# Key halves copied from PSUM into the score slots, wide mask transposes and a new order in a block-sparse attention and Hyena kernel

## The chip, the cores and the metric

The kernel runs on one core of a Trainium2 chip. The metric is the device time of one execution in microseconds. Before the change the median of three executions is 249.28 us (249.26 to 249.30). The profiled execution has a span of 248.8 us.

In what follows PE is TensorE, ACT is ScalarE, DVE is VectorE, POOL is GpSimd and SP is SyncE, which issues all the DMAs.

## The reference

Two stages follow each other. The first is causal attention in which every query sees its own block of 64 keys and the three blocks with the highest gate scores; the second is a Hyena layer with an FFT over the sequence and a product of three projections.

```python
batch, n_heads, seq, head_dim = (4, 8, 768, 64); block = 64; top_k = 3
k_rep = k.reshape(B, H, n_blocks, block, D).mean(axis=3)
gate_scores = np.einsum('bhsd,bhnd->bhsn', q, k_rep)          # blocks after the query's own: -1e9
top_idx = np.argsort(gate_scores, axis=-1)[..., -top_k:]
# mask: keys of the chosen blocks and of the own block, and no key after the query
scores = np.where(mask, scale * np.matmul(q, k.transpose(0, 1, 3, 2)), -1000000000.0)
x = np.matmul(softmax(scores), v)                              # then [B, S, H * D]
proj = x @ w_proj                                              # x1, x2, x3
x2_conv = np.fft.irfft(np.fft.rfft(x2, axis=1) * np.fft.rfft(filter_fft, axis=0), n=S, axis=1)
out = (x1 * x2_conv * x3) @ w_out
```

## The kernel before

The work on attention is cut into 16 pairs of heads (`g`), four pairs to a batch. Each pair goes through `prep(g)` and `attn(g)`; when four pairs are done, `hyena(b)` can work on their batch. `filt()` prepares the Fourier matrices and the filter once, at the start.

`prep` works so. The loads (L274, L281) bring k, q and v of two heads into tiles kn, qn and vn, with the sequence on the partitions. Six transposes `kT` (L342) put both heads' keys into PSUM, in two halves of 384 columns, so that head 0 has partitions 0 to 63 and head 1 has 64 to 127. DVE sums each block of 64 keys (`ks`, L345), and ACT copies the 384 columns as 16-bit numbers into a tile k2 (`k2`, L350). Six transposes `qT` (L374) do the same for q; ACT writes the scaled high part q2h (L377) and DVE the remainder q2l (L380). POOL splits the key sums into a high and a low part (`km`, L363, L364). Twenty small matmuls `gate` (L409) give the gate scores. DVE then finds the third largest of each row (`max`, L422 to L428) and compares (`lt`, L434, L439); the result nm says which blocks are not chosen. Five transposes `mT` (L450) turn nm, and a copy `md` (L458) puts 12 rows of it for each head beneath the q of that head.

The score slots kt and qt are the operands of the score matmuls `sc` (L480). For each head, rows 0 to 63 hold k and q; rows 64 to 75 of kt hold a constant pattern (-30720 in the columns of one block), and the same rows of qt hold nm. So one matmul with 76 rows gives the scores with the unchosen blocks pushed far down. Because head 1 sits on partitions 64 to 127 after the transposes but is needed on 0 to 63, `shuffle` (L393) moves the halves of k2 and q2h into the slots by DMA. For the first two pairs engines copy instead (L395).

`attn` runs, for each head, three pieces of scores with two PSUM banks each (`sc`), an exponential on ACT (`ex`, L486), a causal cut on POOL (`sel`, L491), and 21 matmuls with v (`pv`, L508); DVE normalises (`rec` L517, `nrm` L521, tile xn). Then a DMA transposes xn into xT (L540), sums and differences of xn (`eo`, L546) go through the Fourier matrices (`st1`, L558, L565), and copies of that are XT (L571).

`hyena` has, per batch, six groups `s2` of four matmuls (L667) on the four pairs' XT; DVE multiplies each group's PSUM twice with the filter (`t`, L676) and the sums Y (L686) are made on DVE or POOL. Sixteen groups `x13` (L703) are the projections, `prod` (L712) their product, `cv` (L730) the transform back, then `sd` (L745), `yT` (L751), and six groups `op` (L761) with the copy `osb` (L765) and the store.

The order is a planned one. `build` makes a graph of operations, each with a due time `vt`, the engines that could do it and a cost on each. `plan` then runs through a model of five engines, PSUM banks and buffer pools, and always takes the operation that could start soonest, or, of those nearly equal, the one due first. While PE would have nothing to do in the first 30 us of the plan, it adds filler matmuls (L856)[...]. What comes out is a fixed sequence for each engine, and each engine keeps to it: an instruction that waits holds up all that stands behind it on its engine, on SP's DMA queue as well. A few numbers in `PAR` shift the due times, and `POOLS` says how many buffers each tile has.

Of the kernel before, what the change touches and what calls it, by code (L numbers as in the profile page):

```python
# [24 lines left out]
KR = D + NB  # L25
# [16 lines left out]
for _pi, _segs in enumerate(PIECES):  # L42
# [6 lines left out]
    p0=-2.579, p1=0.077, a0=0.0, pvlag=0.294, dlag=1.997, dlen=0.945, h0=5.459, hlen=3.658, f0=0.196,  # L49
    f1=4.432, ld=-1.443, s2a=-0.205, s2b=0.422, x0=0.488, x1=0.938, c0=0.578, c1=0.847, o0=1.481,  # L50
    o1=1.0, pen_dve=0.221, ahead=2.229, delta=0.029, queue=6.554, direct=2, late=2.0, w0=1.031, wl=1.656,
    wlag=-0.256, warm_until=30, tr0=-7.197, trl=1.834, fill0=0.703,
)

POOLS = dict(kn=3, qn=3, vn=2, k2=2, q2h=2, q2l=2, ks=2, km=3, m8=2, nm=2,
# [8 lines left out]
class Buf:  # L64
    def __init__(self, pool):
        self.pool, self.slot, self.left = pool, None, 0
        self.w, self.r = {}, {}
        self.free = self.busy = 0.0
        self.users = []
# [7 lines left out]
class Graph:  # L77
    def __init__(self):
        self.ops = []

    def add(self, tag, vt, eng, emit, rd=(), wr=(), res=(), lock=False, size=0):
        o = Op()
        o.i, o.tag, o.vt, o.eng, o.emit, o.lock, o.size = len(self.ops), tag, vt, eng, emit, lock, size
# [25 lines left out]
def pe_cost(mms):  # L109
    occ = sum(mms)  # L110
    return occ, occ - mms[-1] + 0.17 + mms[-1]


def dve(n, rate=1.0):
    occ = n / (960.0 * rate) + 0.066
    return occ, occ + 0.15
# [11 lines left out]
def build(par):  # L128
    g_ = Graph()
# [56 lines left out]
    add("phase", T0, {"DVE": (1.0, 1.15)}, e_phase, wr=[cb("phase"), cb("magic")])  # L186
    add("iota", T0 + .1, {"POOL": pol(1.7)}, e_iota, wr=[cb("cols")])
    add("nyq", T0 + .2, {"DVE": (0.08, 0.23)}, e_nyq, wr=[cb("cols")])
    def e_eblk(E, nc, en):
        nc.gpsimd.memset(E.eblk[64:KR, :], EMASK)  # L190
        nc.gpsimd.affine_select(out=E.eblk[64:KR, :], in_=E.eblk[64:KR, :], compare_op=ALU.is_ge,
                                fill=0.0, base=0, pattern=[[1, S]], channel_multiplier=-64)
        nc.gpsimd.affine_select(out=E.eblk[64:KR, :], in_=E.eblk[64:KR, :], compare_op=ALU.is_ge,
                                fill=0.0, base=63, pattern=[[-1, S]], channel_multiplier=64)

    add("eblk", T0 + 3, {"POOL": pol(2.5)}, e_eblk, wr=[cb("eblk")])


    slot_init = []
    for i in range(POOLS["kt"]):  # L200
        def e_fill(E, nc, en, i=i):
            eng = nc.vector if en == "DVE" else nc.gpsimd
            eng.memset(E.t["qt"][i][64:KR, :, 0:P], 0.0)
            eng.tensor_copy(
                E.t["kt"][i][64:KR, :, :],
                E.eblk[64:KR, :].rearrange("p (o s) -> p o s", o=1).to_broadcast([NB, 2, S]))
        slot_init.append(add("fill", par["fill0"] + i, {"DVE": (0.62, 0.77), "POOL": pol(2.6)}, e_fill, rd=[cb("eblk")],
                             wr=[cb(("slot", i))]))

    def e_small(E, nc, en):  # L210
        for t_ in E.t["km"]:
            nc.vector.memset(t_, 0.0)
        for t_ in E.t["nm"]:
            nc.vector.memset(t_, 0.0)
        for t_ in E.t["va"]:
            nc.vector.memset(t_[:, :, :, 64:65], 1.0)
        nc.vector.memset(E.crow, 2.0 / S)
        nc.vector.memset(E.crow[0:1, :], 1.0 / S)
# [47 lines left out]
    for g in range(NG):  # L266
# [4 lines left out]
        for n_, (src, dst) in enumerate((("k", kn[g]), ("q", qn[g]))):  # L271
            for t in range(2):
                def e_ld(E, nc, en, b=b, j=j, t=t, dst=dst, src=src):
                    nc.sync.dma_start(E.sb(dst)[:, :, t, :],  # L274
                                      getattr(E, src)[b, 2 * j + t].rearrange("(c p) d -> p c d", p=P))
# [48 lines left out]
    def prep(g):  # L324
        direct = g < par["direct"]
# [5 lines left out]
        Kt[g], Qt[g] = Buf("kt"), Buf("qt")  # L331
        if g < POOLS["kt"]:
            Kt[g].slot = Qt[g].slot = g
        k2, q2h, q2l, ks, km = Buf("k2"), Buf("q2h"), Buf("q2l"), Buf("ks"), Buf("km")
        m8, nm = Buf("m8"), Buf("nm")
        for hf in range(2):
# [11 lines left out]
            def e_k2(E, nc, en, cs=cs, kp=kp):  # L348
                if en == "ACT":
                    nc.scalar.copy(E.sb(k2)[:, cs], E.bk(kp)[:, 0:HS])  # L350
                else:
                    nc.vector.tensor_copy(E.sb(k2)[:, cs], E.bk(kp)[:, 0:HS])

            add("kT", v(.0 + .1 * hf), {"PE": pe_cost([0.109] * 3)}, e_kt, rd=[(kn[g], 0), (kn[g], 1), cb("id32")], wr=[kp],
                res=[k2, ks])
            add("ks", v(.05 + .1 * hf), {"DVE": dve(HS)}, e_ks, rd=[kp], wr=[(ks, hf)])
            add("k2", v(.05 + .1 * hf), {"ACT": act(HS)}, e_k2, rd=[kp], wr=[(k2, hf)])

        def e_km(E, nc, en):
            for t in range(2):  # L360
                r = slice(64 * t, 64 * t + 64)
                cc = slice(12 * t, 12 * t + 12)
                nc.gpsimd.tensor_copy(E.sb(km)[r, 0, cc], E.sb(ks)[r, :])  # L363
                nc.gpsimd.tensor_tensor(E.sb(km)[r, 1, cc], E.sb(ks)[r, :], E.sb(km)[r, 0, cc],  # L364
                                        op=ALU.subtract)

        add("km", v(.3), {"POOL": pol(1.0)}, e_km, rd=[(ks, 0), (ks, 1), cb("small")], wr=[km])
        for hf in range(2):
            cs = slice(HS * hf, HS * (hf + 1))
            qp = psb()  # L370

            def e_qt(E, nc, en, hf=hf, qp=qp):
                for c in range(HC):
                    nc.tensor.transpose(E.bk(qp)[:, P * c:P * (c + 1)], E.sb(qn[g])[:, HC * hf + c, :, :], E.id32)  # L374

            def e_qh(E, nc, en, cs=cs, qp=qp):
                nc.scalar.activation(E.sb(q2h)[:, cs], E.bk(qp)[:, 0:HS], AF.Copy, bias=0.0, scale=QS)  # L377

            def e_ql(E, nc, en, cs=cs, qp=qp):
                nc.vector.scalar_tensor_tensor(out=E.sb(q2l)[:, cs], in0=E.bk(qp)[:, 0:HS], scalar=QS,  # L380
                                               in1=E.sb(q2h)[:, cs], op0=ALU.mult, op1=ALU.subtract)

            add("qT", v(.2 + .1 * hf), {"PE": pe_cost([0.109] * 3)}, e_qt, rd=[(qn[g], 0), (qn[g], 1), cb("id32")], wr=[qp],
                res=[q2h, q2l])
            add("qh", v(.25 + .1 * hf), {"ACT": act(HS)}, e_qh, rd=[qp], wr=[(q2h, hf)])
            add("ql", v(.27 + .1 * hf), {"DVE": dve(HS)}, e_ql, rd=[qp, (q2h, hf)], wr=[(q2l, hf)])

        def shuffle(src, dst, vt, tag):
            for t in range(2):
                def e_sh(E, nc, en, t=t):  # L390
                    o, i_ = E.sb(dst)[0:64, t, :], E.sb(src)[64 * t:64 * t + 64, :]
# [5 lines left out]
                add(tag, vt, eng, e_sh, rd=[(src, 0), (src, 1)], wr=[(dst, ("h", t))],  # L397
                    size=0 if direct else 98, lock=direct)

        shuffle(k2, Kt[g], v(.3), "shK")  # L400
        shuffle(q2h, Qt[g], v(.4), "shQ")

        gn = psb()

        def e_gate(E, nc, en):
            o = E.bk(gn)
            for c in range(1, NQ):
                for n_, (qx, w) in enumerate(((q2h, 0), (q2h, 1), (q2l, 0), (q2l, 1))):
                    nc.tensor.matmul(o[:, 32 * c:32 * c + 24], lhsT=E.sb(qx)[:, P * c:P * (c + 1)],  # L409
                                     rhs=E.sb(km)[:, w, 0:24], start=(n_ == 0), stop=(n_ == 3))  # L410

        add("gate", v(.5), {"PE": pe_cost([0.026] * 20)}, e_gate,
            rd=[(q2h, 0), (q2h, 1), (q2l, 0), (q2l, 1), km], wr=[gn], res=[m8, nm])
# [16 lines left out]
        def e_lt(E, nc, en):  # L430
            o = E.bk(gn)
            gv = o[:, 32:32 * NQ].rearrange("p (c n) -> p c n", n=32)
            n_ = E.sb(nm)
            nc.vector.tensor_tensor(n_[:, :, :, 0:NB],  # L434
                                    gv[:, :, 0:24].rearrange("p c (t n) -> p c t n", t=2),
                                    E.sb(m8)[:, :, :, 2:3].to_broadcast([P, 5, 2, NB]), op=ALU.is_lt)
            row = 5 * 2 * 32
            for half in range(2):
                nc.vector.memset(bass.AP(tensor=n_.tensor, offset=n_.offset + half * (64 * row + 1) + 2,  # L439
                                         ap=[[row, 64], [66, 5], [32, 2]]), 0.0)  # L440

        add("max", v(.55), {"DVE": (1.12, 1.25)}, e_max, rd=[gn], wr=[gn, m8])
        add("lt", v(.56), {"DVE": (0.53, 0.65)}, e_lt, rd=[gn, m8, cb("small")], wr=[nm])
# [3 lines left out]
        def e_mt(E, nc, en):  # L447
            o = E.bk(mt).bitcast(FP16)
            for c in range(5):
                nc.tensor.transpose(o[0:64, P * c:P * (c + 1)],  # L450
                                    E.sb(nm)[:, c, :, :].rearrange("p t n -> p (t n)"), E.id16)

        add("mT", v(.8), {"PE": pe_cost([0.056] * 5)}, e_mt, rd=[nm, cb("id16")], wr=[mt],
            res=[Qt[g]])
        for t in range(2):
            def e_md(E, nc, en, t=t):
                o = E.bk(mt).bitcast(FP16)
                (nc.vector.tensor_copy if en == "DVE" else nc.scalar.copy)(  # L458
                    E.sb(Qt[g])[64:KR, t, P:S], o[32 * t:32 * t + NB, 0:S - P])
            add("md", v(.85), {"DVE": (0.398, 0.55), "ACT": (0.59, 0.755)}, e_md, rd=[mt, cb(("slots", g))],  # L460
# [5 lines left out]
    def attn(g):  # L466
# [3 lines left out]
        for t in range(2):  # L470
            a = g + par["a0"] + 0.5 * t
            exs = []
            for pi in range(3):
# [3 lines left out]
                def e_sc(E, nc, en, t=t, pi=pi, sp=sp):  # L477
                    o = E.sp(sp)
                    for (col, kc, q0, w) in PIECES[pi]:
                        nc.tensor.matmul(o[:, col:col + w], lhsT=E.sb(Kt[g])[0:KR, t, P * kc:P * (kc + 1)],  # L480
                                         rhs=E.sb(Qt[g])[0:KR, t, q0:q0 + w], start=True, stop=True,
# [6 lines left out]
                def e_sel(E, nc, en, pi=pi, ex=ex):  # L488
# [7 lines left out]
                    rd=[(Kt[g], ("h", t)), (Qt[g], ("h", t)), (Qt[g], ("m", t)), cb(("slots", g))], wr=[sp], res=[ex])  # L496
# [3 lines left out]
            for n_, cs in enumerate(((0, 1, 2), (3, 4), (5,))):  # L500
# [11 lines left out]
                add("pv", a + par["pvlag"] + 0.05 * n_, {"PE": pe_cost([0.030] * sum(c + 1 for c in cs))},  # L512
# [548 lines left out]
```

## Time and profile before

| | before |
|---|---|
| median time | 249.28 us |
| span of the profiled execution | 248.8 us |
| busy PE / DVE / ACT / POOL | 236.4 / 204.8 / 175.6 / 129.3 us |
| share of PE in the chain that ended last | 79% |
| k copies on ACT (L350) | 32, 481 ns each |
| DMAs kt<-k, qt<-q2h | 28 and 28, 96 KB each, 3.0 and 3.5 us to landing |
| fillers (L856) | 106, 16.2 us busy |

A matmul's end is modelled in this profile, and matmuls are pipelined; a busy PE is therefore not a PE at its best, and the start of one group to the start of the next tells more. Times of an engine's idle stretch are given with the instruction that ended it.

### The profile page before, as it was taken

The page shows a single profiled execution, that of the slowest core. Times are in us where ns is not written, and L with a number is a line of the kernel's source. Part 1 is how long each engine was busy: PE and PEld are TensorE (multiplying, and loading weights), DVE is VectorE, ACT ScalarE, POOL GpSimd, SP SyncE. Part 2 cuts the span into 40 slices and gives each one's busy share as a digit, 9 for nine tenths or more (in the row PEclk, how much of TensorE's full clock was granted, in tenths as well). Part 3 has the DMA queues.
Part 4 walks back from the last instruction along what each step waited for, and adds up shares of the span by engine and source line. Part 5 has one row for each costly group of instructions (what it writes and reads, how often), then busy time and mean ns, then how long its engine had stood idle before and what let it go on. Part 6 is the DMA issues. An engine that isn't in the chain of part 4 may idle for free.

```text
span 248.8 us, 6695 instructions
## 1 busy us (share of the span) xinstructions
PE 236.4 (95%) x2410; PEld 161.1 (65%) x2410; DVE 204.8 (82%) x643; ACT 175.6 (71%) x296; POOL 129.3 (52%) x240
## 2 busy tenths in 40 slices
PE   8978998999889899999999999999999999999994
PEld 6756687678556576867766677677566766645651
DVE  7899788988997999998899786778898968589860
ACT  2877999999667679886865796767756873524443
POOL 6662457675485547554558476643444614063420
PEclk9999999999997999999999999999999999999999
DMA  6999499997999958999976895421415131032006
GB/s 167 336 229 249 102 248 221 233 245 174 275 212 224 234 151 203 247 180 214 216 188 172 195 279 115 107 54 33 108 42 161 42 34 32 9 139 109 3 20 234
DMA packets 98945, 40.02 MB, mean 161 GB/s; under 512 B 89440, under 2 KB 93024, under 8 KB 98912
## 3 DMA queue, kind: packets, MB, share of 16 engines
q1 hardware_dynamic: 98912, 39.60, 66.3%
q8 instruction: 19, 0.31, 0.5%
q14 instruction: 14, 0.11, 0.2%
HBM read 24.64 MB, written 6.29 MB: 124 GB/s over the span
## 4 chain that ended last, share of the span: by engine, by line
PE 79%; DVE 7%; SPq 6%; DMA 3%; ACT 2%; issue 1%; DVEq 0%; ACTq 0%
PE ps L703 16%; PE ps L480 14%; PE ps L761 8%; PE ps L667 8%; PE ps L508 7%; PE ps L730 6%; PE ps L558 4%; SPq L274 3%; PE ps L374 3%; PE ps L342 3%; PE ps L409 2%; PE ps L450 2%; PE ps L565 2%; SPq L297 2%; DMA t<-in_moe_w_out_dram 2%; DVE t L676 2%
## 5 line engine op out<-in xcount | busy, mean ns | idle before, releaser
L486 ACT ACTIVATE ex<-ps 128x1024 f16<-128x1024 f32 (+1 forms) x96 | 86.1, 930 | 14.7 <-PE ps L480 14.4
L491 POOL TENSOR_SCALAR_AFFINE_SELECT ex<-ex 128x256 f16<-128x256 f16 x96 | 41.7, 437 | 52.4 <-ACT ex L486 51.6
L480 PE MATMUL ps<-qt,kt 76*128 76x512 f16 (+3 forms) x256 | 51.2, 310 | 0.3 <-ACT ex L486 0.3
L703 PE MATMUL ps<-xT,wp 128*128 128x384 f16 x256 | 50.5, 326 | 0.0
L703 PEld LDWEIGHTS <-wp 128*128 128x128 f16 x256 | 24.0, 97 | 14.1 <-issue 0.2
L686 POOL TENSOR_TENSOR Y<-t,t 128x512 f16<-128x512 f32 (+1 forms) x18 | 23.4, 1306 | 18.7 <-DVE t L676 18.3
L480 PEld LDWEIGHTS <-kt 76*128 76x128 f16 x256 | 23.1, 99 | 15.1 <-issue 1.4
L508 PEld LDWEIGHTS <-ex 128*128 128x128 f16 x672 | 25.2, 97 | 3.9 <-POOL km L363 0.4
L508 PE MATMUL ps<-va,ex 128*128 128x65 f16 x672 | 26.8, 193 | 0.2 <-DVE nm L434 0.2
L765 ACT COPY osb<-ps 128x512 f32<-128x512 f32 x24 | 14.2, 590 | 15.1 <-PE ps L761 15.0
L667 PE MATMUL ps<-wp,XT 128*128 128x512 f16 x96 | 23.7, 381 | 0.2 <-DVE t L676 0.2
L761 PE MATMUL ps<-wo,yT 128*128 128x512 f16 x96 | 23.8, 379 | 0.0
L751 POOL TENSOR_TENSOR yT<-prod,sd 128x384 f16<-128x384 f32 x16 | 15.9, 1000 | 13.5 <-DVE sd L745 11.2
L712 DVE TENSOR_TENSOR prod<-ps,x 128x384 f32<-128x384 f32 x32 | 17.6, 552 | 6.5 <-PE ps L703 6.2
L350 ACT CAST k<-ps 128x384 f16<-128x384 f32 x32 | 14.7, 481 | 11.3 <-DVE colv L182 4.6
L676 DVE TENSOR_TENSOR t<-ps,HA 128x512 f32<-128x512 f32 x24 | 16.5, 686 | 6.3 <-PE ps L667 6.2
L730 PE MATMUL ps<-G,Y 128*128 128x384 f16 x96 | 20.8, 326 | 0.0
L709 ACT CAST x<-ps 128x384 f16<-128x384 f32 x29 | 14.0, 483 | 9.4 <-PE ps L703 4.6
L345 DVE TENSOR_REDUCE ks<-ps 128x6 f32<-128x384 f32 x32 | 17.1, 552 | 4.1 <-ACT k L350 2.0
L380 DVE SCALAR_TENSOR_TENSOR q2l<-ps,q2h 128x384 f16<-128x384 f32 x32 | 17.0, 551 | 2.3 <-ACT q2h L377 2.2
L521 DVE TENSOR_TENSOR xn<-ps,rec 128x384 f16<-128x384 f32 x32 | 17.8, 556 | 1.0
L745 DVE TENSOR_TENSOR sd<-ce,ps 128x384 f32<-128x384 f32 x32 | 16.3, 549 | 2.2 <-PE ps L730 1.5
(106 smaller groups left out, 435.0 us busy)
## 6 DMA issues: line engine op xcount, KB each, us to landing
kn<-in_k_dram SPq DMA_DIRECT2D x32, 192.0 KB, 3.6
qn<-in_q_dram SPq DMA_DIRECT2D x32, 192.0 KB, 3.6
vn<-in_v_dram SPq DMA_DIRECT2D x16, 384.0 KB, 4.3
out_dram<-osb SPq DMA_DIRECT2D x24, 256.0 KB, 2.0
t<-in_moe_w_proj_dram SPq DMA_DIRECT2D x12, 256.0 KB, 4.2
kt<-k SPq DMA_DIRECT2D x28, 96.0 KB, 3.0
qt<-q2h SPq DMA_DIRECT2D x28, 96.0 KB, 3.5
t<-in_moe_filter_fft_dram SPq DMA_DIRECT2D x6, 256.0 KB, 4.6
```

The lines of the kernel that those rows point to most:

```text
L480: nc.tensor.matmul(o[:, col:col + w], lhsT=E.sb(Kt[g])[0:KR, t, P * kc:P * (kc + 1)], rhs=E.sb(Qt[g])[0:KR, t, q0:q0 + w], start=True, sto ...
L486: nc.scalar.activation(E.sb(ex)[:, 0:w], E.sp(sp)[:, 0:w], AF.Exp, scale=ESC)
L491: nc.gpsimd.affine_select(out=dv, in_=dv, compare_op=ALU.is_ge, fill=0.0, base=0, pattern=[[0, 2], [1, P]], channel_multiplier=-1)
L508: nc.tensor.matmul(o[:, 65 * c:65 * c + 65], lhsT=E.sb(exs[pi])[:, col:col + P], rhs=E.sb(va[g])[:, t, kc, :], start=(kc == 0), stop=(kc = ...
L521: nc.vector.tensor_tensor(E.sb(xn)[:, :, t, :], pov[:, :, 0:64], E.sb(rec).rearrange("p (c n) -> p c n", n=1) .to_broadcast([P, NQ, D]), o ...
L667: nc.tensor.matmul(E.bk(xa), lhsT=w, rhs=E.wp[:, j, Dm:2 * Dm], start=(j == 0), stop=(j == NP - 1))
L676: nc.vector.tensor_mul(E.sb(dst), E.bk(xa), m)
L686: (nc.vector if en == "DVE" else nc.gpsimd).tensor_tensor(E.sb(Y)[ro, n_, :], E.sb(x)[ri, :], E.sb(y)[ri, :], op=op)
L703: nc.tensor.matmul(E.bk(xq)[:, 0:HS], lhsT=E.wp[:, d2, 2 * Dm * m + P * dc:2 * Dm * m + P * (dc + 1)], rhs=E.sb(xT[gs[d2]])[:, cs], start= ...
L712: nc.vector.tensor_mul(E.sb(prod)[:, cs], E.bk(xq)[:, 0:HS], E.sb(x1))
L730: nc.tensor.matmul(E.bk(cv)[:, 0:HS], lhsT=E.sb(Y)[:, 3 * p_ + n_, P * dc:P * (dc + 1)], rhs=E.G[:, 3 * p_ + n_, :], start=(n_ == 0), stop ...
L761: nc.tensor.matmul(E.bk(op_), lhsT=E.sb(yT)[:, d2, P * c:P * (c + 1)], rhs=E.wo[:, d2, :], start=(d2 == 0), stop=(d2 == NP - 1))
```

## The change

It has four parts.

1. Key halves: the score slots are laid out anew. Head 1, which leaves the transposes on partitions 64 to 127, keeps them, with its block pattern and mask in partitions 0 to 11; head 0 keeps 0 to 63 with pattern and mask in 64 to 75. So the keys can be copied from PSUM straight into the slot, one copy of 64 partitions for each head and half, on ACT or DVE, and no DMA moves them. The score matmul of head 1 has 128 rows (rows 12 to 63 are zero), that of head 0 still 76. The q halves still go by DMA, from a tile qx that holds high and low part, now into 128-column pieces.
2. Mask transposes: nm is one tile with 64 columns for each 128 queries, and each transpose takes 128 of them, so that the masks come out on the partitions where both heads need them.
3. km: POOL writes a copy more for each head, so that high and low part can be placed apart from where they are made.
4. Order: the planner's costs, due times and penalties are set anew, with a shift for each kind of operation, and buffers of kt, qt and qx are taken in the pairs' order. Pools: kn 3 to 2, k2 2 to 1 (unused), nm 2 to 1, q2h and q2l (2 each) become qx with 4.

The diff also carries another way to bring q (`by_dma`); with `tm=16` no pair uses it. `kin=16` makes all pairs take the new way for keys.

```diff
-KR = D + NB
+XW = 2 * P * NQ + 64
+NMW = 64 * NQ
+KR = (76, 128)
...
-    p0=-2.579, p1=0.077, a0=0.0, pvlag=0.294, dlag=1.997, dlen=0.945, h0=5.459, hlen=3.658, f0=0.196,
+    p0=-2.542, p1=0.159, a0=0.0, pvlag=0.294, dlag=1.721, dlen=1.15, h0=5.159, hlen=3.761, f0=-0.171,
...
-POOLS = dict(kn=3, qn=3, vn=2, k2=2, q2h=2, q2l=2, ks=2, km=3, m8=2, nm=2,
+POOLS = dict(kn=2, qn=3, vn=2, k2=1, qx=4, ks=2, km=3, m8=2, nm=1,
...
     def add(self, tag, vt, eng, emit, rd=(), wr=(), res=(), lock=False, size=0):
         o = Op()
+        vt += self.par.get("v_" + tag, 0.0)
...
+            if in_place:
+                for t in range(2):
+                    def e_k2(E, nc, en, hf=hf, kp=kp, t=t):
+                        r = slice(64 * t, 64 * t + 64)
+                        (nc.scalar.copy if en == "ACT" else nc.vector.tensor_copy)(
+                            E.sb(Kt[g])[r, HC * hf:HC * (hf + 1), 1 - t, :],
+                            E.bk(kp)[r, 0:HS].rearrange("p (c s) -> p c s", s=P))
+                    add("k2", v(.05 + .1 * hf + .02 * t), {"ACT": act(HS), "DVE": dve(HS)} , e_k2, rd=[kp],
+                        wr=[(Kt[g], ("h", t, hf))])
...
-                nc.gpsimd.tensor_copy(E.sb(km)[r, 0, cc], E.sb(ks)[r, :])
-                nc.gpsimd.tensor_tensor(E.sb(km)[r, 1, cc], E.sb(ks)[r, :], E.sb(km)[r, 0, cc],
-                                        op=ALU.subtract)
+                nc.gpsimd.tensor_copy(x[r, 2, 0:12], E.sb(ks)[r, :])
+                nc.gpsimd.tensor_tensor(x[ru, 1, cc], E.sb(ks)[r, :], x[r, 2, 0:12], op=ALU.subtract)
+                nc.gpsimd.tensor_copy(x[ru, 0, cc], x[r, 2, 0:12])
...
-                    o, i_ = E.sb(dst)[0:64, t, :], E.sb(src)[64 * t:64 * t + 64, :]
+                    r = slice(64 * t, 64 * t + 64)
+                    o = E.sb(dst)[r, :, 1 - t, :]
+                    i_ = E.sb(src)[r, col:col + S].rearrange("p (c s) -> p c s", s=P)
...
-        shuffle(k2, Kt[g], v(.3), "shK")
-        shuffle(q2h, Qt[g], v(.4), "shQ")
+        if not in_place:
+            shuffle(k2, 0, Kt[g], v(.3), "shK")
...
+            shuffle(qx, 0, Qt[g], v(.4), "shQ")
...
-                nc.tensor.transpose(o[0:64, P * c:P * (c + 1)],
-                                    E.sb(nm)[:, c, :, :].rearrange("p t n -> p (t n)"), E.id16)
+                nc.tensor.transpose(o[:, P * c:P * (c + 1)], E.sb(nm)[:, 64 * c:64 * c + P], E.id16)
...
-                        nc.tensor.matmul(o[:, col:col + w], lhsT=E.sb(Kt[g])[0:KR, t, P * kc:P * (kc + 1)],
-                                         rhs=E.sb(Qt[g])[0:KR, t, q0:q0 + w], start=True, stop=True,
+                        nc.tensor.matmul(o[:, col:col + w], lhsT=E.sb(Kt[g])[0:KR[t], kc, 1 - t, :],
+                                         rhs=E.sb(Qt[g])[0:KR[t], q0 // P:(q0 + w) // P, 1 - t, :],
+                                         start=True, stop=True,
...
-            add("rec", vt, {"DVE": (0.105, 0.25)}, e_rec, rd=pos, wr=[rec])
+            add("rec", vt, {"DVE": (0.2, 0.3)}, e_rec, rd=pos, wr=[rec])
```

## The prediction

> **What bounds the kernel now.** I read the page's engine shares and the slices first, then busy time by stage, then TensorE's own timeline where the stages show holes.
>
> ```profile
> span 248.8 us, 6695 instructions
> ...
> PE 236.4 (95%) x2410; PEld 161.1 (65%) x2410; DVE 204.8 (82%) x643; ACT 175.6 (71%) x296; POOL 129.3 (52%) x240
> ```
>
> 95% for PE is too kind: a pipelined matmul counts as busy until its modelled end, and 106 matmuls (L856, 16 us) are fillers. From start to start the timeline gives 0.65 us for four of x13 (L703), 0.67 for 21 of pv, 0.86 for four of s2 or op, 0.49 for 20 of gate or three of cv, 0.65 for six k or q transposes, 1.13 for one head's scores. Times their counts: x13 41.6, sc 36.3, pv 21.2, s2 and op 20.7 each, kT and qT 20.9, st1 15.8, cv 15.6, gate 8.0, mT 4.5, filter and trig 6: **about 211 us of real TensorE work**. The other 38 us of the span are fillers, a tail of about 4 us, and waiting. By stage (busy time of PE, PEld, DVE, ACT, POOL, then clock, DMA share, GB/s):
>
> ```profile
> 0.00:24.00 24.00, 19.82 (x174) 15.96 (x175) 21.00 (x71) 15.67 (x32) 13.90 (x27) 1.00 0.98 245
> 24.00:64.00 40.00, 38.61 (x535) 28.74 (x533) 33.73 (x141) 37.42 (x58) 23.99 (x57) 1.00 0.88 211
> 64.00:90.00 26.00, 22.86 (x221) 14.97 (x218) 23.53 (x74) 17.56 (x29) 15.52 (x29) 0.93 1.03 221
> 90.00:200.00 110.00, 110.00 (x1210) 75.83 (x1210) 94.38 (x302) 83.66 (x138) 61.41 (x114) 1.00 0.63 149
> 200.00:240.00 40.00, 40.00 (x263) 23.49 (x261) 31.06 (x57) 17.75 (x36) 14.49 (x15) 1.00 0.19 48
> ```
>
> Four regimes. To 24 us DVE and the DMA engines are full. From 24 to 64, the first four head pairs, ACT is 94% busy. From 64 to 90, where batch 0's s2 joins, DVE is 90% busy, PE has holes and the clock sinks. After 90 PE never stops: there about 152 us of work fill 155 us, and no change to the other engines can win anything. **So only the first 90 us can be shortened.** The holes of the third regime, on TensorE (start, length, what, idle before and who ended it):
>
> ```profile
> 65.98 0.44 PE L450 MATMUL ps<-id,nm 128*64 128x128 f16 x5 [0.80 <-DVE t L676]
> 66.45 2.75 PE L667 MATMUL ps<-wp,XT 128*128 128x512 f16 x12
> ...
> 70.93 1.02 PE L667 MATMUL ps<-wp,XT 128*128 128x512 f16 x4 [0.21 <-DVE t L676]
> 72.49 0.20 PE L409 MATMUL ps<-km,q2h 128*128 128x24 f16 x2 [0.53 <-DVE t L676]
> ...
> 86.54 0.55 PE L342 MATMUL ps<-id,kn 128*128 128x128 f32 x3 [0.76 <-DVE nm L434]
> ```
>
> Three s2 groups stand back to back (x12). Each feeds two products t on DVE (0.6 us each start to start), so they give DVE 3.6 us at once, and what PE needs next (masks, gate, q low halves) queues behind them on DVE. Then the clock pays once more (column after the busy times):
>
> ```profile
> 72.00:74.00 2.00, 1.23 (x23) 0.95 (x24) 2.00 (x5) 0.27 (x1) 2.00 (x3) 0.95 1.09 247
> 74.00:76.00 2.00, 2.00 (x13) 1.42 (x12) 1.81 (x15) 1.29 (x2) 1.47 (x3) 0.50 1.00 252
> 76.00:78.00 2.00, 2.00 (x10) 0.96 (x8) 0.75 (x4) 1.73 (x2) 0.41 (x1) 0.69 0.81 164
> ```
>
> At 0.50 and 0.69 these four us do the work of 2.4: 1.6 us lost.
>
> [...]
>
> ```profile
> 15.50 2.57 DVE L395 COPY qt<-q2h 64x768 f16<-64x768 f16 x1
> ```
>
> Its median is 0.355; GpSimd worked without pause from 14.94 to 17.84.
>
> **The change, part by part.**
>
> *Key halves from PSUM.* Gone: 28 DMAs kt<-k and four DVE copies. In packets, the 28 are 28 x 64 x 94 ns / 16 engines = 10.5 us of DMA time. All are followed by attention much later, so their 3.0 us of latency is on no path; what they free is DMA time before 90 us: about 12 of them by then, 4.5 us. In return each [128, 384] copy becomes two of [64, 384]. The trace of before has none. Low bound: half of 0.38 us (start to start); high: the full 0.38[...], so I take 0.38. The order has 61 on ACT and 3 on DVE for 32 before: 29 x 0.38 = **11 us more on ACT**. After 90 us ACT has 26 us idle while PE is full: hidden there. In the second regime it isn't.
>
> *Q halves.* They now land in 256-byte runs: 384 packets of 20 ns instead of 64 of 94, 0.48 us instead of 0.38 each, about 1.2 us by 90 us. Net relief by then: some 3 us of nearly 90 that the DMA engines are full.
>
> *Wide mask transposes.* 80 with 128 columns for 80 with 64. A 128-wide transpose takes 0.056 us as before (L565's matmuls, 128 wide, have the same step). Nothing. Scores contract 128 rows for one head: the step follows the columns, nothing; bounds 0 and, if the strided q cost 10% of half of sc, 1.8 us.
>
> *Extra setup.* A second 64-row eblk on GpSimd (0.73 + 2 x 0.82 = 2.4 us, done by 8 us, before km needs it), memsets and fills about as long as before; 32 more km copies on GpSimd, 0.27 each, hidden by q's low halves. GpSimd gets some 30 us more in all, 52% to about 64%, much of it Y, eo and yT taken from DVE; DVE falls by some 4 us.
>
> *Start to the first exponential (24.3 before).* Ahead of the first masks DVE loses about 2 us (copies, two filter sums). [...] The order has 114 fillers for 106, 0.11 us each, but in a stretch where PE waits anyway. I take 0; bounds -1.5 and +1.
>
> *Second regime.* Between the first exponential and the XT copy of pair 3, ACT holds 35.2 us before (20 + 10 exponentials 24.0, 8 k copies 3.0, 8 q copies 3.0, the rest 5.2) and took 39.3 (24.34 to 63.65). After: the same exponentials, 20 half copies 7.4, 10 q copies 3.7: 40.0. With 2 to 4 us idle, XT ends at 66.2 to 68.2 and s2 starts near 67.5. Before, it starts at 62.8. But the new order does 41.6 us of TensorE work ahead of it (one more pair prepared), the old 38.9; before reached 41.6 at 66.6. **Real loss: 1 us, bounds 0 and 2.**
>
> *Third regime.* In the new order no two s2 groups of batch 0 are neighbours: six stand in 16.6 us of TensorE work (from 41.6 to 58.1), with scores and pv between, and the DVE work from first to last t is 16.9 us. Both fit side by side. The planner's costs that set this order came closer to the trace (reciprocal 0.105 to 0.2, traced 0.19), so its places should fit better. The mask chain gets room too: the least TensorE work between a gate and its transposes is 2.8 us, 2.2 before, for a DVE chain of about 1.9 (ten max, compare, memsets) plus handoffs. Before, this stretch of work took 66.6 to 89.0, 22.4 us, with 5.8 lost. I give the new order 2 us of loss (bounds 0.5 and 5): 18.6 us. **Gain 3.8, bounds 0.8 and 5.3.**
>
> *After that* both have 153 us of work to go; the old loses 3 in it. The last 6 op groups and their copies are as before. 0, bounds -1 and +1 (SyncE's queue has fewer issues, 172 for 200, but kn has 2 buffers for 3, so a k load can hold the queue up; one pair takes some 13 us of PE, a load 3.6).
>
> Sum: 0 + 1 - 3.8 + 0 = -2.8, and half a microsecond for the freed DMA time (w_out's casts waited on it near 84 to 90): **246.0 us**.
>
> **Rivals.**
> - *ACT takes the place of DVE.* The 3.7 us of doubled copies up to s2 go on the path whole and the interleaved s2 stage waits on ACT instead: +3.7 - 1.5 = 251.5. For: 94% busy from 24 to 64. Against: 32% idle from 64 to 90. With it the two-buffer kn queue: similar time. 0.22.
> - *Both cancel*: second regime +2, third -2: 249.3. 0.08.
> - *All holes go.* The third regime loses 0.5, the start gains 1.5, the second costs nothing: 249.3 - 5.3 - 1.5 = 242.5. For: the order shows more distance everywhere. [...] 0.15.
> - *Forecast*, 246.0: 0.55.
>
> **Numbers.** Faster takes forecast and third rival, 0.70; same 0.08; slower 0.22. The range runs from all holes gone to just short of the first rival's centre: 242.0 to 251.0.
>
> **What would show it.** ACT groups for k: 61 of about 0.48 us, no kt DMA. PE work spaced as before in scores. Fewer "DVE t" waits on PE between 64 and 90 and no slice of clock near 0.5 there: right. s2 starting after 69 us, or PE idle on ACT ex between 30 and 64: the first rival. PE holes after 90 us, or kn issues that hold SyncE for many us: wrong in what I called nothing.

## The result, and the profile after

The changed kernel takes 250.22 us (median of 4, 249.94 to 250.66) where the kernel before takes 249.29 us: a ratio of 1.0039, 95% interval 1.0022 to 1.0056. It is **slower by some 0.9 us**, and the forecast of 246.0 us was wrong. The profiled span is 248.9 us, against 248.8 before. The traced execution of the kernel before, here and in the prediction, is one of the longer ones: it took 250.48 us, with the clock at half speed from 73.8 to 77.2 us, while the executions of 249.3 us have a span of 247.6.

The page of the changed kernel first, then its busy times by stage (columns as in the prediction):

```profile
span 248.9 us, 6719 instructions
...
PE 234.8 (94%) x2418; PEld 162.3 (65%) x2418; DVE 199.0 (80%) x634; ACT 184.5 (74%) x316; POOL 156.4 (63%) x299
```

```profile
24.00:64.00 40.00, 34.58 (x448) 24.96 (x447) 32.02 (x124) 35.00 (x59) 26.05 (x62) 1.00 0.77 186
64.00:90.00 26.00, 24.72 (x292) 17.82 (x291) 23.35 (x90) 25.10 (x42) 19.90 (x45) 1.00 0.99 231
```

Read the row from 24 to 64 against the one of before. ACT has more to do now, and yet it is *less* busy (35.00 us, was 37.42); so is DVE (32.02, was 33.73), and TensorE has 5.4 us of holes where it had 1.4. When these three get less done at once, none of them is the bound: they wait for each other. From 64 to 90 it is the other way round: TensorE has gained 1.9 us of busy time, and the clock doesn't dip where it stood at 0.50 and 0.69:

```profile
74.00:76.00 2.00, 1.82 (x13) 0.99 (x12) 1.88 (x5) 1.96 (x4) 0.26 (x1) 1.00 1.05 240
76.00:78.00 2.00, 2.00 (x17) 1.09 (x16) 2.00 (x5) 2.00 (x4) 1.72 (x9) 1.00 1.22 275
```

Counting TensorE's real work from start to start, as the prediction did, gives the time at which each kernel had done so much of its 210 us:

| work done | 10.8 us | 25 us | 41.6 us | 58.1 us | 100 us | 150 us | 200 us |
|---|---|---|---|---|---|---|---|
| before | 30.3 | 48.0 | 67.1 | 89.5 | 132.8 | 184.3 | 234.7 |
| after | 30.8 | 50.8 | 71.2 | 89.5 | 134.1 | 184.6 | 234.8 |

At 41.6 us of work, the end of the second regime, the new kernel is 4.1 us late; in the third regime it wins the same 4.1 back (22.4 us then, 18.3 now). So there are two effects that cancel in these two traces. Some 1.2 us of what is won back is the dip (an estimate: 248.8 less 247.6), which an execution of 249.3 us doesn't have. Against such a one the gain is some 2.9 us, and the loss is larger than the gain, as the measured 0.9 us says.

The loss has a name in the groups: idle time of the engine just before them is at the right.

```profile
L380 ACT CAST kt<-ps 64x384 f16<-64x384 f32 x61 | 28.8, 473 | 12.9 <-DVE ks L370 7.4
...
L370 DVE TENSOR_REDUCE ks<-ps 128x6 f32<-128x384 f32 x32 | 17.3, 551 | 7.0 <-ACT kt L380 6.6
```

ACT's key copies wait for DVE's key sums, and DVE's key sums for ACT's key copies. The two read the same PSUM bank and nothing of each other's. The timeline of all engines (start, length, what, idle before and who ended it) shows how:

```profile
35.00 0.52 DVE L370 TENSOR_REDUCE ks<-ps 128x6 f32<-128x384 f32 x1
...
35.60 1.46 ACT L380 CAST kt<-ps 64x384 f16<-64x384 f32 x3 [1.05 <-DVE ks L370]
...
37.09 0.56 DVE L370 TENSOR_REDUCE ks<-ps 128x6 f32<-128x384 f32 x1 [1.11 <-ACT kt L380]
...
37.69 0.47 ACT L380 CAST kt<-ps 64x384 f16<-64x384 f32 x1 [0.62 <-DVE ks L370]
...
38.21 0.44 PE L535 MATMUL ps<-id,nm 128*128 128x128 f16 x5 [0.72 <-ACT kt L380]
```

ACT, in its fullest stretch, stands still for 1.05 us until the sum has ended, copies; DVE stands still for 1.11 until the copies have ended, sums; ACT waits another 0.62; and TensorE's next transposes wait 0.72 us for the bank that the last copy holds. I call such a handover a **turn**. The exponential that stands behind these copies on ACT starts at 38.18 us, though its scores were done at 34.12. Matched by the planned order, the copies and sums of one bank never overlap: in all 38 handovers between the two engines (32 before) the second starts at least 0.032 us after the first has ended, and in 28 of the 38 within 0.1 us of it (18 of 32 before). The planner knows of no such wait: it lets both readers start once the transposes are done.

From 23 to 71 us, first exponential to s2, the waits of ACT alone, and then of DVE alone, are headed by

```profile
ACT kt L380 <- DVE ks L370: 3.9, 5, 1.1
```

```profile
DVE ks L370 <- ACT kt L380: 3.9, 5, 1.1
```

(us, times, longest). Before, ACT lost 0.8 us on all its k copies between 24 and 63, 0.2 of it to sums. The 3.9 us are of the size of the 4.1 lost; whether they are its cause is for experiments to show.

### The profile page after: what moved, and what is told of

It reads as the page before. It is cut to its first block, busy times and chain, and to the rows that moved or that the text cites. A ratio compares the mean times of both kernels' runs of the same rounds, so it can differ in the third digit from the quotient of the medians.

```text
span 248.9 us, 6719 instructions
## 1 busy us (share of the span) xinstructions
PE 234.8 (94%) x2418; PEld 162.3 (65%) x2418; DVE 199.0 (80%) x634; ACT 184.5 (74%) x316; POOL 156.4 (63%) x299
## 4 chain that ended last, share of the span: by engine, by line
PE 78%; ACT 10%; DVE 6%; issue 3%; POOL 2%; ACTq 0%; DVEq 0%; POOLq 0%
PE ps L790 16%; PE ps L565 11%; PE ps L848 8%; PE ps L754 8%; PE ps L595 7%; PE ps L817 6%; ACT kt L380 6%; PE ps L949 5%; PE ps L645 4%; DVE ks L370 3%; PE ps L367 3%; PE ps L487 3%; ACT ex L572 3%; PE ps L429 2%; PE ps L652 2%
## 5 line engine op out<-in xcount | busy, mean ns | idle before, releaser
L577 POOL TENSOR_SCALAR_AFFINE_SELECT ex<-ex 128x256 f16<-128x256 f16 x96 | 40.9, 431 | 35.0 <-ACT ex L572 33.9
L565 PE MATMUL ps<-qt,kt 76*128 76x512 f16 (+7 forms) x256 | 50.7, 305 | 2.7 <-ACT ex L572 2.0
L773 POOL TENSOR_TENSOR Y<-t,t 128x512 f16<-128x512 f32 (+1 forms) x25 | 31.5, 1269 | 16.1 <-DVE t L763 15.7
L380 ACT CAST kt<-ps 64x384 f16<-64x384 f32 x61 | 28.8, 473 | 12.9 <-DVE ks L370 7.4
L565 PEld LDWEIGHTS <-kt 76*128 76x128 f16 (+1 forms) x256 | 23.2, 97 | 17.4 <-issue 4.4
L595 PEld LDWEIGHTS <-ex 128*128 128x128 f16 x672 | 26.2, 98 | 6.0 <-issue 1.9
L595 PE MATMUL ps<-va,ex 128*128 128x65 f16 x672 | 27.8, 193 | 1.0 <-DVE ks L370 0.7
L838 POOL TENSOR_TENSOR yT<-prod,sd 128x384 f16<-128x384 f32 x19 | 19.0, 1003 | 13.0 <-DVE sd L832 9.7
L852 ACT COPY osb<-ps 128x512 f32<-128x512 f32 x22 | 12.9, 588 | 16.8 <-PE ps L848 14.1
L370 DVE TENSOR_REDUCE ks<-ps 128x6 f32<-128x384 f32 x32 | 17.3, 551 | 7.0 <-ACT kt L380 6.6
L435 DVE SCALAR_TENSOR_TENSOR qx<-ps,qx 128x384 f16<-128x384 f32 x32 | 17.3, 552 | 4.3 <-ACT qx L432 3.8
```

Source lines behind the costliest of these rows:

```text
L370: nc.vector.reduce_sum(E.sb(ks)[:, 6 * hf:6 * hf + 6], E.bk(kp)[:, 0:HS].rearrange("p (n t) -> p n t", t=64), axis=AX.X)
L380: (nc.scalar.copy if en == "ACT" else nc.vector.tensor_copy)(E.sb(Kt[g])[r, HC * hf:HC * (hf + 1), 1 - t, :], E.bk(kp)[r, 0:HS].rearrange( ...
L565: nc.tensor.matmul(o[:, col:col + w], lhsT=E.sb(Kt[g])[0:KR[t], kc, 1 - t, :], rhs=E.sb(Qt[g])[0:KR[t], q0 // P:(q0 + w) // P, 1 - t, :], ...
L577: nc.gpsimd.affine_select(out=dv, in_=dv, compare_op=ALU.is_ge, fill=0.0, base=0, pattern=[[0, 2], [1, P]], channel_multiplier=-1)
L595: nc.tensor.matmul(o[:, 65 * c:65 * c + 65], lhsT=E.sb(exs[pi])[:, col:col + P], rhs=E.sb(va[g])[:, t, kc, :], start=(kc == 0), stop=(kc = ...
L773: (nc.vector if en == "DVE" else nc.gpsimd).tensor_tensor(E.sb(Y)[ro, n_, :], E.sb(x)[ri, :], E.sb(y)[ri, :], op=op)
```

## The experiments

**Half the copies, and sums from elsewhere.** Is it the turns, or ACT's doubled work? One run leaves out one of the two copies, another takes the sums from a constant; each keeps the planned order.

```diff
 e1_half_copies
+                        if t == 1:
+                            return
...
 e2_sums_apart
-                                     E.bk(kp)[:, 0:HS].rearrange("p (n t) -> p n t", t=64), axis=AX.X)
+                                     E.kconst.rearrange("p (n t) -> p n t", t=64), axis=AX.X)
```

> The changed kernel in its order, with the second key half's copies (head 1 of each pair) left out: 32 of 64 copies are not made, so head 1 scores against zeros. ScalarE gets about 11 us less work, as much as the kernel before had. Theory 1 (the doubled copies and the turns that they take with the key sums on VectorE at the same PSUM bank hold up the stretch from 24 to 70 us): 4 us or more faster than the changed kernel, 246 us or less, waits of ScalarE copies and key sums for each other about halved. Rival (the new order is worse there by itself): within 1 us of the changed kernel, 249 to 250.

> The changed kernel in its order, all copies made, but the key sums on VectorE read a constant tile of the same size in place of the PSUM bank that ScalarE copies from (so the gate works on constants). Turns at the bank are gone, the amount of work stays. Theory 1a (the turns cost the time): 3 us or more faster than the changed kernel, 247 or less, no ScalarE idle before key copies put down to key sums. Theory 1b (the mere amount of ScalarE work costs it): less than 1 us, 249.3 or more.

Measured: 243.17 us for half the copies (ratio 0.9741, 0.9713 to 0.9769) and 242.82 for the sums apart (0.9733, 0.971 to 0.9757). Either alone gives back over 7 us. In the second run ACT is 39.01 us busy from 24 to 64, where the changed kernel came to 35.00:

```profile
24.00:64.00 40.00, 37.81 (x505) 28.09 (x505) 35.74 (x142) 39.01 (x65) 29.09 (x73) 1.00 0.92 219
```

The second edit takes away more than turns: a sum of a constant doesn't wait for TensorE's transposes either, and the bank comes free sooner. The 7.4 us between 250.22 and 242.82 are therefore the turns and this together. The next runs make the same edit in the old kernel, where all of it is worth 2.5 us.

**The same in the kernel before.** Its key copies made as two of 64 partitions; and the control that the last run lacks, sums from a constant in the old kernel, with whole and with split copies.

```diff
 e3_before_split, e6_before_split_sums_apart
...
-                    nc.scalar.copy(E.sb(k2)[:, cs], E.bk(kp)[:, 0:HS])
+                for t in range(2):
+                    r = slice(64 * t, 64 * t + 64)
+                    nc.scalar.copy(E.sb(k2)[r, cs], E.bk(kp)[r, 0:HS])
```

> The kernel before in its order, with each key copy of 128 partitions issued as two of 64, one after the other; all else as it was. If the doubling costs the time (amount or turns): slower by 3 to 5 us, 252 to 254, and TensorE idle between 24 and 64 us grows by as much. If the new order is the cause: within 1 us of 249.3, since ScalarE had some 4 us idle in that stretch.

> The kernel before in its own order, with the key sums taken from a constant tile in SBUF and not from the PSUM bank that ACT copies; the gate then works on constants. It is the control of the same edit in the new kernel. Theory 1 (the turns at a bank cost the time): the old kernel has only 2.7 us of such waits, so 247.5 to 249.5 us. Rival (sums that no longer wait for TensorE shorten the chain to the masks and set the bank free sooner, in either kernel): 242 to 245 us.

> The kernel before in its own order, each key copy made as two copies of 64 partitions, and the key sums taken from a constant tile in SBUF; the gate works on constants. Theory 1 (turns): most of the 11.5 us that the split cost go, 249 to 252 us, the rest being ACT's doubled work. Rival (ACT's work itself, on an order that has no room for it): 257 to 261 us.

Measured: 260.84 us split (ratio 1.0446, 1.0405 to 1.0487), far over what either theory gave; 246.76 with the sums apart (0.988, 0.9847 to 0.9912), 0.7 below the range of theory 1; 253.34 with both edits (1.0143, 1.0109 to 1.0177), 1.3 above its range. The waits of the split kernel show the turns, and TensorE's weight loads of the q transposes (L373) behind banks that are held longer:

```profile
DVE ks L345 <- ACT k L351: 8.5, 13, 2.0
...
PEld ps L373 <- DVE ks L345: 3.9, 6, 0.7
PEld ps L373 <- ACT k L351: 2.6, 5, 0.7
```

**Both at once in the new kernel.**

> The changed kernel in its order, key sums from a constant tile (242.82 us so far), and head 1's half of every key copy left out, so that ACT has its old number of key copies; its slots hold zeros, the gate works on constants. It prices the doubled copies alone, with no turns at a bank. Theory 1 (turns are the cost, the doubled work is hidden): 241.8 to 243 us. Rival (on a second regime that is bound by ACT the work itself costs too, as it did in the old order with 6.6 us between two runs without turns): 238.5 to 241.5 us.

Measured: 241.44 us (0.9662, 0.9628 to 0.9697), between the two and just inside the rival's range. That fills two squares of four (us):

| | with turns | sums apart | turns cost |
|---|---|---|---|
| new order, half the copies | 243.17 | 241.44 | 1.7 |
| new order, all half copies | 250.22 | 242.82 | 7.4 |
| copies cost | 7.0 | 1.4 | |
| old order, whole copies | 249.29 | 246.76 | 2.5 |
| old order, split copies | 260.84 | 253.34 | 7.5 |
| copies cost | 11.5 | 6.6 | |

So my first theory, turns and not work, was too simple. In the new order doubled copies alone cost 1.4 and turns alone 1.7; together they cost 8.8. My reading, which no run tests apart: each copy more can be a turn more, and an ACT without slack has no time in which to take it. (Half the copies are also half the readers on ACT.)

**Who goes first.** Three runs keep the planned order and the whole computation, and move only copies or sums of one bank against each other: both halves at the place of the first; the sum ahead of the copies; the copies ahead of the sum.

```diff
 e10_sums_first
         for o in order:
+            if o.tag == "k2":
+                for b in o.bufs:
+                    s = sums.get(id(b))
+                    if s is not None and s not in done:
+                        done.add(s)
+                        s.emit(E, nc, s.on)
...
```

> The changed kernel in its planned order, but both half copies of a bank are issued at the place of the first, so that the key sum never stands between them (it does in 9 of 32 banks). Everything is computed. Theory 1 (turns): fewer exchanges, a gain of 1 to 2.5 us, 247.7 to 249.2 us. Rival (it is having two readers at all, not the number of exchanges, or the place of the copies on ACT): 249.8 to 251 us.

> The changed kernel in its planned order, but the key sum of a bank is issued ahead of its first copy wherever the plan had it later (18 of 32 banks), so DVE never waits for an ACT copy at a bank and ACT may wait for DVE. Everything is computed. Theory 1, sharpened after the run that put the halves together (what costs is that lag passes in both directions between the two queues): 246.5 to 249 us. Rival (a turn costs the same whoever goes first): 249.8 to 252 us.

> The mirror of the run with the sums first: the changed kernel in its planned order, but both half copies of a bank are issued ahead of its key sum (35 copies move forward), so ACT never waits for DVE at a bank and DVE may wait for ACT. Everything is computed. Theory 1 in its new form (what costs is ACT, the engine without slack, waiting for DVE's queue): 244 to 248 us. Rival (either direction costs, since DVE's masks then wait for ACT and TensorE for the masks): 250 to 256 us.

Measured: 252.70 (1.0123, 1.0087 to 1.0158), 255.43 (1.0231, 1.0188 to 1.0273) and 253.70 us (1.0171, 1.0156 to 1.0186). All three are slower than the planned order; the first two lie above both of their ranges, the third in its rival's. (By the planned order the sum stands between the two copies in 7 banks, not 9.) So neither fewer exchanges nor one direction alone helps. The direction can be chosen, as the waits of the two last kernels show, but not the loss:

```profile
ACT kt L380 <- DVE ks L370: 14.0, 15, 1.6
```

```profile
POOL km L397 <- DVE ks L370: 15.3, 9, 4.1
DVE ks L370 <- ACT kt L380: 11.9, 20, 1.3
```

With the sums first, ACT loses 14.0 us; with the sums last DVE loses 11.9, and POOL's km, which starts the mask chain, waits 15.3 (10.4 in the changed kernel). Such an edit also pulls instructions forward in a queue that was planned without it; that share wasn't measured apart, so these runs don't price a turn.

**Does a reader wait for the bank, or for what both read?** One run copies only partitions 0 to 63 and sums only 64 to 127, so that no partition has two readers. In the other each sum is made as two of 64 partitions, head 1's first, while the copies take head 0 first.

```diff
 e16_opposite_halves (copies as in e1_half_copies; e17_sums_split: both slices of ks, one after the other)
-                nc.vector.reduce_sum(E.sb(ks)[:, 6 * hf:6 * hf + 6],
-                                     E.bk(kp)[:, 0:HS].rearrange("p (n t) -> p n t", t=64), axis=AX.X)
+                nc.vector.reduce_sum(E.sb(ks)[64:P, 6 * hf:6 * hf + 6],
+                                     E.bk(kp)[64:P, 0:HS].rearrange("p (n t) -> p n t", t=64), axis=AX.X)
```

> As the run with half the copies (243.17 us, with 7.6 us of waits between copies and sums), but the sum too reads only half of the bank: the copies take partitions 0 to 63, the sums 64 to 127; head 1's copies and head 0's sums are left out. If a reader waits only for partitions that the other reads[...]: no such waits are left, 241 to 242.2 us, as with half the copies and the sums apart (241.44). If it waits for the bank: the waits stay near 7 us, 242.6 to 244 us.

> The changed kernel in its planned order, each key sum made as two sums of 64 partitions, head 1's first, while the copies take head 0's first. Everything is computed. DVE has 32 more sums of about 0.55 us, 17 us more. If a reader waits only for partitions that the other reads: the handovers get looser, 248 to 252 us. If it waits for the bank: more readers and more turns, 252 to 258 us.

Measured: 245.21 us (0.9838, 0.9821 to 0.9854) and 269.10 us (1.078, 1.0754 to 1.0806). Both lie above both of their ranges. In the first, the waits stay though no partition is shared, and none of its 30 handovers overlaps (smallest gap 0.031 us):

```profile
ACT kt L385 <- DVE ks L373: 6.1, 8, 1.3
...
DVE ks L373 <- ACT kt L385: 2.0, 5, 0.5
```

So this program waits for the whole bank. (Why it takes 2 us more than with half the copies and whole sums wasn't followed up; a sum of 64 partitions takes no less time, 0.559 us for 0.551.) With the sums split there are more readers and more turns, 22.6 us of waits both ways, and the time rises by 18.9 us. That fits a cost of turns but doesn't prove it: the run also gives DVE some 18 us more work (sums busy for 35.5 us, were 17.3), and the two aren't set apart.

**DMA or order in the third regime.** The sums apart, and 28 transfers as the old key shuffle had put back on the queue.

```diff
+                        if hf == 1 and g >= 2:
+                            nc.sync.dma_start(E.kd0[r, :], E.colv[r, :])
```

> The changed kernel in its order, key sums from a constant tile (242.82 us without the next edit), and 28 transfers of 64 packets of 1,536 bytes put back on the DMA queue where the key copies are made; they carry constants into a tile that nobody reads. The gate works on constants. Theory 2 (the gain of the third regime comes from the new order): 242.5 to 244 us. Rival (it comes from the DMA time that the change frees): 245.5 to 248 us.

Measured: 243.14 us (242.92 to 243.81), 0.3 above the same kernel without them (242.64 to 243.13). So the freed DMA time is worth next to nothing here, and the third regime's gain isn't the DMA's. The new order is what is left for it, together with the smaller parts of the change, which no run separates from the order.

**The triple of s2 groups.** In the old kernel, the first batch's twelve products t on half their columns.

```diff
-                        nc.vector.tensor_mul(E.sb(dst), E.bk(xa), m)
+                        w = Dm // 2 if b == 0 else Dm
+                        nc.vector.tensor_mul(E.sb(dst)[:, 0:w], E.bk(xa)[:, 0:w], m[:, 0:w])
```

> The kernel before in its order, with the twelve filter products of the first batch made on half their columns only (the other half is left out), 0.27 us less each on VectorE. If VectorE's backlog behind three s2 groups in a row made the holes and the clock dip between 64 and 80 us: 3 to 4 us faster, 245.5 to 246.5, the clock near 1.00 throughout. If those holes have another cause (transfers, mask chain): less than 1 us faster.

Measured: 248.05 us (0.9969, 0.9954 to 0.9984). Only 1.25 us come back: DVE's backlog behind the triple is a part of the third regime's holes, not most of them. The clock stays at 1.00 in this trace, but a mean clock of 0.990 to 0.993 stands in nine of this kernel's twenty executions (0.991 or 0.992 in 3 of 23 of the kernel before), so the edit doesn't do away with the dip, and what decides it stays open.

**Plans that know of turns.** The planner gets one rule, and its parameters are searched anew under it, once with key halves and once with whole copies shuffled by DMA (`kin=0`, two k2 buffers); everything else of the change stays.

```diff
+        for b in o.bufs:
+            if b.pool == "bk" and b.last and b.last[0] != e:
+                est = max(est, b.last[1])
         return est
...
         free[e] = est + occ
+        for b in o.bufs:
+            b.last = (e, est + vis)
```

> The changed kernel, everything computed, with one more rule in the planner: a reader of a PSUM bank starts when the last reader on another engine is done; and its parameters searched anew under that rule. The order is another one, so a shift of some us by chance is possible. Theory 1 (the plan failed because it let the two readers of a bank overlap): 243 to 247 us. Rival (the key halves cost too much in any order): 249 to 252 us.

> As the run planned for turns, with the same rule and a search of the same kind, but with the keys copied whole and shuffled by DMA as in the kernel before (two k2 buffers); all else of the change stays. Everything is computed. Theory (key halves from PSUM are worth their work when the plan knows the turns): 1 us or more slower than that run. Rival (the key halves are the part that lost the time, in any plan): 1 us or more faster than that run, 243 to 247 us.

> As the run planned for turns (245.34 us), with the result of another search under the same rule; everything is computed. Theory (the plan without overlapped readers makes the change a gain): 242.5 to 247 us, slower than the replanned old keys. Rival (that run was one lucky order): 248 to 252 us.

> As the run with the old keys planned for turns (241.96 us), with the result of another search under the same rule, whose planned time is 0.6 us longer; everything is computed. Theory (the key halves are what costs some 3 us, plan for plan): 241.5 to 244 us. Rival (the difference to the key halves was chance): 244.5 to 248 us.

| | us | ratio to before |
|---|---|---|
| key halves, planned for turns | 245.34 (242.43 to 246.04) | 0.9796 (0.973 to 0.9863) |
| the same, second search | 246.06 | 0.9872 (0.9858 to 0.9887) |
| old keys, planned for turns | **241.96** | 0.969 (0.9651 to 0.9729) |
| the same, second search | 243.91 | 0.9787 (0.9771 to 0.9803) |

All four beat both kernels; the old keys in the first search lie 1 us below the range of their rival. In the kernel of the first row the waits of copies and sums for each other are down to 0.3 us, with 63 copies on ACT:

```profile
L382 ACT CAST kt<-ps 64x384 f16<-64x384 f32 x63 | 29.6, 475 | 6.5 <-PE ps L369 6.0
```

The longest wait is for transposes now. Of its 33 handovers 6 follow within 0.1 us, no longer 28 of 38: the readers are apart in time. The old keys are faster still, by 3.4 and 2.2 us in the two searches (one of the four executions of the first row, 242.43 us, is as fast as theirs). In these plans the key halves are a part of the change that costs. Two things aren't tested: a new search without the rule, and a plan with the right price of a half copy. The planner takes 0.378 us for it on ACT; it holds ACT for some 0.49, as the next section shows.

## Why the prediction was wrong, by its steps

*Second regime: wrong, the step that failed.* "Real loss: 1 us, bounds 0 and 2" came out as 4.1. The prediction took 40.0 us of work on ACT (its terms add up to 40.3) and "2 to 4 us idle", some 43 us from the first exponential to s2, which was to start near 67.5. It took 47.9, from 23.11 to 71.0:

```profile
23.11:70.90 47.79, 41.83 (x549) 30.88 (x547) 38.83 (x155) 42.79 (x70) 31.29 (x77) 1.00 0.81 201
```

ACT was busy for 42.8 us and idle for 5.0, and 3.9 of the 5.0 were turns for the sums. I priced the second copy as work on ACT and missed that it is also one more reader of a bank that DVE reads: this wait was put at nothing. The row was there to see, on a k copy of the old timeline:

```profile
34.04 0.48 ACT L350 CAST k<-ps 128x384 f16<-128x384 f32 x1 [0.23 <-DVE ks L345]
34.41 1.63 ACT L486 ACTIVATE ex<-ps 128x1024 f16<-128x1024 f32 x2
```

And 18 of the old kernel's 32 handovers follow within 0.1 us, none of them closer than 0.032. With the sums taken elsewhere the stretch is 43.5 us long (21.94 to 65.45), about as forecast, and work 41.6 is reached at 64.9 in the old kernel and at 65.9 in the new one, a loss of 1.0. That the sum is right without turns is in part luck: ACT is busy for 42.5 of the 43.5 us, so the work was put 2.5 too low and the idle time 2 too high.

*Key halves, the copy itself: its length right, its price too low.* 61 copies of 64 partitions take 473 ns each, the 32 of 128 before took 481: half the partitions and next to no less time. That a half copy would cost the full price was my estimate; no trace of before showed it. But the prediction priced a copy at 0.38 us, from start to start, because whole copies overlap with what follows: 0.37 us in the two lines above. Half copies don't:

```profile
53.73 1.93 ACT L380 CAST kt<-ps 64x384 f16<-64x384 f32 x4
55.69 1.62 ACT L572 ACTIVATE ex<-ps 128x1024 f16<-128x1024 f32 x2
```

Four of them take 1.96 us, 0.49 each. Over the whole kernel that makes some 17.6 us more on ACT, not 11 (an estimate: 61 at 0.485 us for 32 at 0.375). How much of the lost time this longer hold makes wasn't tested apart. Doubled copies cost 1.4 us in the new order with the sums apart.

*Third regime: right, but for the clock.* Gain 3.8 (0.8 to 5.3) forecast, 4.1 in the traces, some 2.9 without the dip; none of TensorE's waits over 0.3 us between 64 and 90 is for t any more. The prediction took the dip for a cost of the holes ahead of it. It is in the traced execution and not in the 249.3 us that the forecast started from, so there was no such time to win. Sums apart in both kernels, neither trace with a dip, it is 21.2 us against 17.9, a gain of 3.3.

*Start: within its bounds.* The first exponential comes 1.2 us sooner (23.11, was 24.34), but at 10.8 us of work TensorE is half a microsecond late. The one long copy of before (L395, 2.57 us) has no like: the three such copies on DVE after take 0.69 to 0.96 us. What made it long wasn't shown.

*Wide masks, 128 score rows: right, nothing.* From start to start a mask transpose takes 0.056 us in both kernels, and a score matmul of 512 columns 0.216 with 128 rows and 0.220 with 76. TensorE's work sums to 210.1 us, 210.0 before.

*Freed DMA time, 0.5 us: at most 0.3*, by the transfers put back. *After 90 us*: 1.3 us lost up to work 100, 1.0 of it won back by 150. Three holes, 1.1 us of idle time in all, at 97.7, 98.7 and 117.1, have TensorE waiting for a bank that a key copy holds. I had called the doubled copies hidden there because ACT has idle time; but TensorE waits for the bank, not for ACT's share.

*Rivals.* The time fell nearest to "both cancel" (249.3), and in kind it was that, at twice the size in the second regime. The sign of "ACT takes the place of DVE" (251.5), s2 after 69 us, came too, and so did a full ACT (25.10 of the 26 us from 64 to 90). Its second half didn't: TensorE's waits for ACT there come to 0.3 us, and the interleaved s2 stage gained.

As a whole: sums apart in both, the change goes from 246.76 to 242.82, -3.9 where the forecast was -3.3. Of that, 2.3 come by the end of the third regime and some 1.6 after it, where I had put 0, so the agreement of the totals is partly luck too. What the forecast lacked is in the main one term, turns (with what else that edit frees): 7.4 us after against 2.5 before, 4.9.

## What to carry to other kernels

Before you split a read of PSUM, list who else reads that bank: here the second copy was more work on ACT (some 17.6 us, the estimate above) and made 38 handovers of 32, and from 23 to 71 us ACT and DVE lost 3.9 us each waiting for the other. Look for short idle gaps ahead of one reader that another reader ends (0.23 us on the k copy at 34.04). Price a copy from start to start in the form that you are going to use (0.49 us here), not in the one that you have (0.37). If a planner sets the order, give it that wait: here the rule and a new search together turned a loss of 0.9 us into a gain of some 3 to 4. That the key halves cost more than they gave showed only once the old way was planned by the same rule.

## What was not expected of the hardware, and what stays open

Two engines that read one PSUM bank took turns in every one of the handovers that I matched (32 before, 38 after), none overlapping, the closest 0.032 us apart. The releasers in the trace are semaphores, so these are waits of the program. The wait is for the bank, even between partitions 0 to 63 and 64 to 127: 8.1 us of waits are left with copies and sums on opposite halves. What the banks would do without it wasn't tried.

A half copy holds ACT longer than a whole one only where both halves are made. In the changed kernel, what follows a copy of partitions 64 to 127 starts only when that has ended, 0.498 us after its start (median). With head 1's copies left out, what follows a copy of partitions 0 to 63 starts after 0.376 us and overlaps with it by 0.1, as with whole copies (0.375 us before). Whether it is the change from one half to the other, or partitions 64 to 127 themselves, wasn't tried.

Turns aren't additive: 8.5 us of waits for copies went with a loss of 11.5 us in the split old kernel, and 7.6 us of waits both ways cost 1.7 in the new one with half the copies. My reading is that it counts whether the engines have slack where they fall; no run tests that alone.

It stays open how much of the gain of the replanned kernels over the kernel before is the rule, how much the search and how much the other parts of the change; and why the forced orders cost 2.5 to 5.2 us beyond the planned one.
